# Attention fused with a gated FFN: the global rows one step later, with the second half of the next chunk's scores directly behind them

**Chip, cores, metric.** One NeuronCore of a Trainium2 chip. The metric is the device time of one execution in microseconds, the median of several; all runs compared here were in the fast state, so none lies more than 1.5% above the fastest of its kernel (or they were single looks, whose state is called unknown), with a granted TensorE clock of 0.998 to 1.0.

## The reference

Attention over 8 batches x 8 heads x 576 positions x 64, with a band of 32 positions to each side and 8 "global" positions that see all and are seen by all; then a gated FFN over the 4608 rows of 512.

```python
scores = q @ k.T / sqrt(64)
mask   = (|i - j| <= 32) | is_global[i] | is_global[j]
x      = softmax(where(mask, scores, -1e9)) @ v            # (4608, 512), heads side by side
ffn    = (gelu(x @ w_gate) * (x @ w_val)) @ w_out          # 512 -> 1536 -> 512
out    = x + sigmoid(x @ w_res) * ffn
```

## The kernel before

The 4608 rows are nine chunks c of 512. While TensorE does the FFN of chunk c, the attention of chunk c+1 is woven into the FFN's output half, as jobs ahead of its sixteen steps. Those steps are, for each of four row tiles t: `gate` (four matmuls `r_ps`, then a tanh) and three `third` (four matmuls `f_ps` each; after the last one VectorE makes `prb`). Cut to what matters (`...` marks cuts):

```python
psm = tile_pool(bufs=4, PSUM)   # "mm": g_ps, v_ps, r_ps, f_ps, scores of heads 4..7, in turn
pss = tile_pool(bufs=2, PSUM)   # "sc": ss, scores of heads 0..3, transposes
psn = tile_pool(bufs=1, PSUM)   # "nd": sg, sn, nd take turns in one tile of two banks

def global_scores(b):           # at the end of the input half
    sg = psn.tile(...)          # global queries against all keys
    for hf in range(2):
        for p in range(NP):     # 32 output rows each: the array in strips of 128*32
            nc.tensor.matmul(sg[32*p:32*p+32, hf, 0:288], kgz[b % 2][:, p, :], qt[b % 2][:, p, ...])
    ss = ...                    # all keys against the global queries, 128*128, 20 matmuls
def global_exp(b, sg, ss): ...  # exp(ss) -> ptg, exp(sg) -> gt, and gt *= maskr on VectorE
def global_rows(b):             # "the global rows"
    sn = psn.tile(...)
    for c in range(-1, 5):
        for p in range(NP):     # outputs of 32 or 16 rows: the array in strips of 128*32
            nc.tensor.matmul(sn[32*p:...], own or ptg, vgb or ve, ...)
    nc.vector.tensor_tensor(vgs, sn, head8, ALU.mult)
def scores(c, quad):            # half of a chunk's scores
    for pp in (0, 1):
        sc = two tiles of pss (pp = 0) or of psm (pp = 1)
        heads(c, quad, pp, sc)  # 16 matmuls of 64 rows and 64 columns: the array in halves of 64*128
    four times: nc.scalar.activation(pt, sc, ACTF.Exp, ...)
    return mask                 # later: pt *= maskw on VectorE
def values(c, t):               # nd = pt @ v (16 matmuls, L575), + gt @ vgs (L587); then xtok = nd / den

        jobs = {n: [] for n in range(16)}
        if c + 1 < NCH:
            if held is not None:                               # c = 1 .. 6
                jobs[0].append(lambda: global_exp(b, *held))
                jobs[3].append(lambda: global_rows(b))
            ...
            jobs[1] += [lambda: half(0), lambda: held_mask[0](0, 4)]
            for t in range(4):
                jobs[5 + 2 * t].append(lambda t=t: values(c + 1, t))
                jobs[7 + 2 * t].insert(0, lambda t=t: turn_x(c + 1, t))   # xtok -> xt, t < 3 by DMA
            jobs[5].append(lambda: half(1))
            jobs[6].append(lambda: held_mask[1](0, 2))
            jobs[7].append(lambda: held_mask[1](2, 4))
        for n in range(16):
            for w in jobs[n]:
                w()
            work_f[n]()
```

The softmax here doesn't subtract the row's maximum and nothing guards it: scores larger than these inputs give would overflow.

## Time and profile before

| | before |
|---|---|
| first three runs | 394.37 us (393.6 to 395.18) |
| span of the profiled run | 392.0 us |
| TensorE, VectorE, ScalarE, GpSimd busy | 97%, 52%, 44%, 43% |
| first `r_ps` of chunk c to that of chunk c+1, c = 1 to 5 | 40.48, 40.80, 40.47, 40.81, 40.48 us |

The lines are in the prediction. The last row, the *pitch* of a chunk, is read off TensorE's timeline and will carry the argument: single executions of one kernel differ by over a microsecond, while the pitches of chunks 1 to 5 repeat to 0.02 us in a second trace of each kernel (e5 and e6). How to read a stream of matmuls: take the start of one group to the start of the next, since the printed durations overlap. What such a step has beyond the matmuls' own time where the array's shape changes is called the *toll*.

### The profile page before, as it was taken

How to read it: one execution, taken by the hardware profiler on the slowest of the kernel's cores; microseconds unless marked ns; L12 is line 12 of the kernel's file. 1: busy time of each engine (PE TensorE's matmuls, PEld its weight loads, DVE VectorE, ACT ScalarE, POOL GpSimd, SP SyncE). 2: the span in 40 equal slices, each digit the busy share in tenths (PEclk: the TensorE clock that was granted, in tenths of full speed). 3: DMA queues.
4: the chain of work that ended last, by engine and by line, in shares of the span. 5: the costliest groups of instructions: out<-in, count | busy, mean ns of one | idle time of the engine just before them, and what ended most of it. 6: DMA issues, size and time to landing. Idle time of an engine off the chain costs nothing.

```text
span 392.0 us, 8491 instructions
## 1 busy us (share of the span) xinstructions
PE 378.8 (97%) x3360; PEld 196.5 (50%) x3360; DVE 203.4 (52%) x446; ACT 171.1 (44%) x285; POOL 169.2 (43%) x203
## 2 busy tenths in 40 slices
PE   3989989999999999999999999999999999999996
PEld 2674555444644454445544554455445544554444
DVE  7767773547543664357444644555445534553422
ACT  6753685236333633354335533462337233633321
POOL 7878764958265424561466137712501210121012
PEclk9999999999999999999999999999999999999999
DMA  8999999699759913997399829992990310041002
GB/s 245 256 378 358 239 321 207 149 196 152 110 97 151 184 42 110 122 204 82 88 149 185 88 82 131 189 113 80 114 150 16 81 55 0 2 93 57 0 28 81
DMA packets 153002, 52.78 MB, mean 135 GB/s; under 512 B 136386, under 2 KB 143426, under 8 KB 152962
## 3 DMA queue, kind: packets, MB, share of 16 engines
q1 hardware_dynamic: 77024, 41.88, 44.4%
q0 software_dynamic: 75392, 9.84, 43.0%
q8 instruction: 26, 0.43, 0.5%
q10 hardware_dynamic: 546, 0.52, 0.4%
q14 instruction: 14, 0.11, 0.1%
HBM read 39.19 MB, written 9.44 MB: 124 GB/s over the span
## 4 chain that ended last, share of the span: by engine, by line
PE 93%; DVE 3%; ACT 2%; issue 1%; POOL 0%; DVEq 0%; POOLq 0%; ACTq 0%
PE g_ps L630 24%; PE v_ps L630 23%; PE f_ps L686 23%; PE r_ps L656 8%; PE nd L575 4%; PE sc L534 3%; PE nd L587 2%; PE ss L481 1%; PE sg L472 1%; PE tx L610 1%; PE tk L451 1%; PE sc L523 1%; PE tq L451 1%; ACT pt L541 1%; PE sn L510 1%
## 5 line engine op out<-in xcount | busy, mean ns | idle before, releaser
L639 DVE SCALAR_TENSOR_TENSOR ht<-gsb,v_ps 128x512 bf16<-128x512 bf16 x108 | 74.2, 688 | 95.3 <-PE v_ps L630 89.2
L636 ACT ACTIVATE gsb<-g_ps 128x512 bf16<-128x512 f32 x108 | 64.4, 597 | 123.1 <-PE g_ps L630 119.7
L692 POOL TENSOR_TENSOR ob<-prb,xtok 128x512 f32<-128x512 f32 x35 | 40.3, 1155 | 172.0 <-DVE prb L690 172.0
L630 PE MATMUL g_ps<-xt,wg_t 128*128 128x512 bf16 (+1 forms) x456 | 111.9, 368 | 0.0
L630 PE MATMUL v_ps<-xt,wv_t 128*128 128x512 bf16 (+1 forms) x456 | 111.9, 368 | 0.0
L686 PE MATMUL f_ps<-wo_t,ht 128*128 128x512 bf16 x420 | 100.1, 379 | 0.0
L630 PEld LDWEIGHTS <-wv_t 128*128 128x128 bf16 x456 | 43.4, 98 | 49.1
L630 PEld LDWEIGHTS <-wg_t 128*128 128x128 bf16 x456 | 43.3, 98 | 48.9 <-issue 0.3
L686 PEld LDWEIGHTS <-ht 128*128 128x128 bf16 x420 | 38.9, 98 | 38.9
L664 ACT ACTIVATE rsb<-r_ps 128x512 bf16<-128x512 f32 x36 | 21.5, 600 | 71.8 <-PE r_ps L656 71.8
L690 DVE SCALAR_TENSOR_TENSOR prb<-rsb,f_ps 128x512 f32<-128x512 bf16 x35 | 24.0, 686 | 27.5 <-PE f_ps L686 26.0
L656 PE MATMUL r_ps<-wr_t,xt 128*128 128x512 bf16 x144 | 36.8, 379 | 1.0 <-ACT rsb L664 1.0
L541 ACT ACTIVATE pt<-sc 128x512 bf16<-128x512 f32 x64 | 33.3, 615 | 4.9 <-PE sc L534 4.8
L91 POOL DMA_DIRECT2D q_st<-in_q_dram x25 | 21.5, 866 | 18.5 <-DMA qt<-q_st 18.4
L557 DVE TENSOR_TENSOR pt<-pt,maskw 128x512 bf16<-128x512 bf16 x56 | 23.2, 424 | 7.7 <-ACT pt L541 5.8
L575 PEld LDWEIGHTS <-pt 128*128 128x128 bf16 x576 | 22.0, 97 | 9.5 <-PE r_ps L656 0.7
L99 POOL DMA_DIRECT2D ve<-in_v_dram x30 | 25.5, 866 | 0.0
L600 DVE TENSOR_TENSOR xtok<-nd,rden 128x512 bf16<-128x512 f32 x34 | 23.5, 691 | 1.3
L91 POOL DMA_DIRECT2D k_st<-in_k_dram x25 | 21.1, 864 | 4.8 <-DMA kt<-k_st 4.1
L575 PE MATMUL nd<-ve,pt 128*128 128x65 bf16 x320 | 22.5, 193 | 0.6 <-DVE xtok L600 0.6
L599 DVE RECIPROCAL rden<-nd 128x8 f32<-128x8 f32 x34 | 7.0, 207 | 29.3 <-PE nd L587 29.2
L656 PEld LDWEIGHTS <-xt 128*128 128x128 bf16 x144 | 13.5, 97 | 16.0 <-issue 0.9
(174 smaller groups left out, 307.9 us busy)
## 6 DMA issues: line engine op xcount, KB each, us to landing
out_dram<-ob SPq DMA_DIRECT2D x35, 256.0 KB
vo<-ve SPq DMA_DIRECT2D x12, 260.0 KB
q_st<-in_q_dram POOLq DMA_DIRECT2D x20, 128.0 KB, 5.8
k_st<-in_k_dram POOLq DMA_DIRECT2D x20, 128.0 KB, 6.5
ve<-in_v_dram POOLq DMA_DIRECT2D x18, 128.0 KB, 7.0
wo_t<-in_k_dram SPq DMA_DIRECT2D x8, 256.0 KB
vraw<-in_q_dram SPq DMA_DIRECT2D x8, 256.0 KB
extra<-in_moe_w_out_dram SPq DMA_DIRECT2D x4, 512.0 KB
```

The source lines that it names most:

```text
L91: nc.gpsimd.dma_start(dst[0:n, r, :].rearrange("p (h d) -> p h d", d=D), src[b].rearrange("h s d -> s h d")[128 * r:128 * r + n])
L99: nc.gpsimd.dma_start(t[p0:p1, c, :, 0:D], v[b].rearrange("h s d -> s h d")[s0 + p0:s0 + p1])
L541: nc.scalar.activation(sc if stay else mine, sc, ACTF.Exp, bias=0.0, scale=SCALE)
L575: nc.tensor.matmul(nds[h // 4][:, VG * (h % 4):VG * (h % 4) + VG], view(pt, 0, 128, c0, [[1, 128]]), vw, start=(h % 4 == 0 and e == 0), st ...
L600: nc.vector.tensor_tensor(xtok[c % 2][:, t, :].rearrange("p (a h d) -> p a h d", a=2, d=D), num[:, :, :, 0:D], view(rden, 0, 128, 0, [[4, ...
L630: nc.tensor.matmul(held[what][:, c0:c1], w[:, kk, 128 * j:128 * j + 128], x[:, kk, c0:c1], start=(kk == 0), stop=(kk == NKT - 1))
L636: nc.scalar.activation(held["s"], held["g"], ACTF.Gelu, bias=0.0, scale=1.0)
L639: nc.vector.scalar_tensor_tensor(ht[:, j, :], held["s"], 0.5, held["v"], ALU.mult, ALU.mult)
L656: nc.tensor.matmul(r_ps, xt[c % 2][:, kk, 128 * t:128 * t + 128], wr_t[:, kk, :], start=(kk == 0), stop=(kk == NKT - 1))
L686: nc.tensor.matmul(held["f"], ht[:, j, 128 * t:128 * t + 128], wo_t[:, j, :], start=(j == 0), stop=(j == NFF - 1))
L690: nc.vector.scalar_tensor_tensor(prb, held["r"], 1.0, held["f"], ALU.add, ALU.mult)
L692: nc.gpsimd.tensor_tensor(ob, prb, xtok[c % 2][:, t, :], ALU.add)
```

## The change

The global rows of chunk c+1 move from ahead of step 3 to ahead of step 4, and the second half of the scores from step 5 to directly behind them. In TensorE's order both small groups now stand side by side, with more room between the exps and the rows that need them.

```diff
--- before.py
+++ after.py
@@ -937,7 +937,7 @@
         if c + 1 < NCH:
             if held is not None:
                 jobs[0].append(lambda: global_exp(b, *held))
-                jobs[3].append(lambda: global_rows(b))
+                jobs[4].append(lambda: global_rows(b))
             held_mask = {}
 
             def half(quad):
@@ -947,7 +947,7 @@
             for t in range(4):
                 jobs[5 + 2 * t].append(lambda t=t: values(c + 1, t))
                 jobs[7 + 2 * t].insert(0, lambda t=t: turn_x(c + 1, t))
-            jobs[5].append(lambda: half(1))
+            jobs[4].append(lambda: half(1))
             jobs[6].append(lambda: held_mask[1](0, 2))
             jobs[7].append(lambda: held_mask[1](2, 4))
         for n in range(16):
```

## The prediction

> **What bounds the kernel now.** I read the page first (busy times, slices, groups), then who waited for whom on TensorE, then the timelines of TensorE, VectorE and ScalarE through the FFN output half of single chunks, which is the only place that the diff touches.
>
> ```profile
> span 392.0 us, 8491 instructions
> PE 378.8 (97%) x3360; PEld 196.5 (50%) x3360; DVE 203.4 (52%) x446; ACT 171.1 (44%) x285; POOL 169.2 (43%) x203
> PE   3989989999999999999999999999999999999996
> PEclk9999999999999999999999999999999999999999
> PE 93%; DVE 3%; ACT 2%; issue 1%; POOL 0%; DVEq 0%; POOLq 0%; ACTq 0%
> ```
>
> TensorE is busy for 97% of the span at full clock and holds 93% of the chain that ended last; no other engine is above 52%. The list of waits for TensorE names only one-off waits, nearly all of the start-up (3.5 us the longest); none recurs once per chunk. So the time can change only by what TensorE's own stream costs, or by a wait that the new order creates. I next look inside that stream, in the chunk whose output half starts at 214.37 us (columns: start, duration from first start to last end, instruction group; repeated lines of L575, sixteen in all, cut):
>
> ```profile
> 214.37 1.02 PE L656 MATMUL r_ps<-wr_t,xt 128*128 128x512 bf16 x4
> 215.33 0.64 PE L534 MATMUL sc<-qt,kt 64*128 64x64 bf16 x32
> 215.90 1.90 PE L686 MATMUL f_ps<-wo_t,ht 128*128 128x512 bf16 x8
> 217.73 0.24 PE L507 MATMUL sn<-vgb,own 128*32 128x130 bf16 x4
> 217.80 0.46 PE L510 MATMUL sn<-ve,ptg 128*16 128x130 bf16 x20
> 218.19 1.04 PE L686 MATMUL f_ps<-wo_t,ht 128*128 128x512 bf16 x4
> 219.06 1.03 PE L656 MATMUL r_ps<-wr_t,xt 128*128 128x512 bf16 x4
> 219.93 0.19 PE L575 MATMUL nd<-ve,pt 128*128 128x65 bf16 x1
> ...
> 220.41 0.39 PE L587 MATMUL nd<-vgs,gt 128*128 128x260 bf16 x2
> 220.73 0.64 PE L534 MATMUL sc<-qt,kt 64*128 64x64 bf16 x32
> ```
>
> Read the differences of the starts, not the durations, which overlap. Four 512-column matmuls take 219.93 - 219.06 = 0.87 us, so 0.216 each. The same four before the scores take 215.33 - 214.37 = 0.96: 0.10 more. Eight before the global rows (`sn`) take 217.73 - 215.90 = 1.83, where 8 x 0.216 = 1.73: again 0.10. The two of L587 before the scores take 0.32; the same two before an f_ps group elsewhere in this chunk take 0.22 (223.53 to 223.75): again 0.10. Leaving such a group costs as much. The last of the 20 `sn` matmuls starts at 217.80 + 0.46 - 0.22 = 218.04 (0.22 is one `sn` matmul), its 130 columns need 0.055 at that rate, yet the next group starts at 218.19: 0.10. The last score matmul starts at 215.33 + 0.64 - 0.19 = 215.78, needs 0.03, and the next starts at 215.90: 0.09. So each time the shape of the array changes (128*128 to 64*128 or to 128*32, or back) the stream loses about 0.10 us. This "idle" is inside what the page counts as busy.
>
> **What the Trainium skill says.** TensorEngine Tiling (Array Packing), section Key Properties: changing the tiling mode, not merely the tile, drains the engine. It gives no time; the trace agrees, at 0.09 to 0.10 us a change as just worked out. Perfetto Trace Analysis, section Tensor Engine Instruction: the end of a matmul in a profile is computed, not observed; that is why I count from starts. ScalarE: Activation LUTs, section What ACT_TABLE_LOAD costs: about 1283 ns; here it is 1.28 us (below), and it matters in the last changed chunk.
>
> **The change part by part.** It applies to seven of the nine chunks (c = 1 to 7); the moved global rows exist in six (c = 1 to 6), as the last has no further batch. No instruction is added or removed. TensorE's order in a chunk was: r, sc, f, f, **sn**, f, r, nd, **sc**, f... and becomes: r, sc, f, f, f, **sn, sc**, r, nd, f... I count the changes of shape. Before: r to sc, sc to f, f to sn, sn to f, nd to sc, sc to f: six. After: r to sc, sc to f, f to sn, sn to sc, sc to r: five. Both small groups now stand together and share one change (128*32 straight to 64*128). Does a change between two small shapes cost one toll or none? Chunk 0 has one, in the other direction:
>
> ```profile
> 52.05 0.64 PE L534 MATMUL sc<-qt,kt 64*128 64x64 bf16 x32
> 52.62 0.24 PE L507 MATMUL sn<-vgb,own 128*32 128x130 bf16 x4
> ```
>
> The last score starts at 52.05 + 0.64 - 0.19 = 52.50 and `sn` at 52.62, the same 0.12 as from scores to f_ps: one ordinary toll. So one toll of 0.10 us is saved in each of six chunks: 6 x 0.10 = 0.6 us.
>
> **New waits, c = 1 to 6.** VectorE works in program order, and there prb of the first row tile now comes before vgs (the copy of `sn`):
>
> ```profile
> 216.64 1.90 DVE L557 TENSOR_TENSOR pt<-pt,maskw 128x512 bf16<-128x512 bf16 x4 [0.52 <-ACT pt L541]
> 218.46 0.69 DVE L514 TENSOR_TENSOR vgs<-sn,head 128x520 bf16<-128x520 f32 x1
> 219.33 0.69 DVE L690 SCALAR_TENSOR_TENSOR prb<-rsb,f_ps 128x512 f32<-128x512 bf16 x1 [0.18 <-PE f_ps L686]
> ```
>
> New times in the same chunk, worked out: f_ps (12) from 215.90 to 218.49, toll to 218.59, `sn` to 219.05 (0.46 with its exit), scores to 219.62 (0.57), r to 220.48, then nd. prb starts 0.27 after its last f_ps slot ends (before: 219.33 against 219.06), so at 218.76, when the masks are done (218.54), and ends at 219.45; vgs runs until about 220.14. The nd matmuls need vgs finished, as `sn` and nd share one PSUM tile: 220.14 against 220.48, a margin of 0.3 us. No wait, but close. The scores' four PSUM tiles were last read by the first half's exps, done at 218.07 (215.99 + 2.08 on ScalarE): no wait at 219.05. After values of tile 0 there is now no score group before the next values: 1.73 us of f_ps against the 0.21 + 0.21 + 0.04 + 0.69 us that VectorE needs to empty nd: no wait.
>
> **c = 7.** Without global rows, four changes stay four (r-sc, sc-f, nd-sc, sc-f become r-sc, sc-f, f-sc, sc-r): no toll saved. But here ScalarE is late, as the table load is not hidden under the previous half:
>
> ```profile
> 337.06 1.28 ACT L541 ACT_TABLE_LOAD   x1
> 338.36 2.06 ACT L541 ACTIVATE pt<-sc 128x512 bf16<-128x512 f32 x4
> 340.58 0.60 ACT L664 ACTIVATE rsb<-r_ps 128x512 bf16<-128x512 f32 x1 [0.16 <-PE r_ps L656]
> ```
>
> The chain that ended last leaves TensorE here: exps to 340.42, a mask 0.44, and nd waits until 340.94, 0.27 us inside its group. The new order delays nd past this, so that wait goes. But the psm ring has four buffers: r, sc, sc, f, and then, in the new order, sc, sc and r. The new r takes the buffer of the first half's fourth score tile, free only when the fourth exp ends, at 340.44. TensorE reaches it at 339.51 + 0.10 + 0.57 = 340.18 and waits 0.27. Then r to 341.31, nd 0.71 to 342.02, f_ps at 342.02; before, f_ps started at 342.02 too. Net 0.
>
> **Sum:** 394.37 - 6 x 0.10 - 0 = 393.8 us (span 392.0 to 391.4).
>
> **Rivals.** (1) *A wait on vgs takes the saving back.* prb ahead of vgs leaves 0.3 us of margin; if vgs ends 0.5 us later than I reckon, nd waits 0.2 six times, +1.2 us: 395.0. For it: the semaphore lags are only read off to about 0.1 us. Against: all durations are in the trace and VectorE is otherwise idle there. (2) *Small shapes follow each other free.* `sn` uses column strips and the scores row halves; if their change is free, two tolls go: 393.2. Against: the chunk 0 lines above. (3) *The change frees a real dependency* (exp to global rows, ScalarE under less pressure): a gain of microseconds. Against it: `sn` starts at 217.73, while gt's mask product ended at 216.12, so it waits for nothing now; the page shows no recurring wait to remove. (4) *The late exps in c = 7 gain or lose* up to 0.3 us, if the ring of buffers turns otherwise than I count. (5) Nothing at all: 394.4.
>
> **Range and chances.** All mechanisms together span 393.2 to 395.0. The three runs of before already span 393.6 to 395.18, so the reading itself adds about half a microsecond: 392.9 to 394.8. Two per cent is 7.9 us, some 13 times the expected gain, and more than every wait that I can construct; the chances outside are for the unforeseen.
>
> **What would show it.** TensorE's timeline after: `sn` directly followed by sc, the sc group 0.12 to 0.15 us behind the last `sn` start; 0.22 instead of 0.32 us for the two L587 matmuls of tile 0; r_ps starts of consecutive chunks about 0.1 us closer. prb before vgs on VectorE, vgs ending 0.3 us before nd starts. In c = 7 the 0.27 us gap inside nd gone and one like it before r_ps. Wrong would be: a wait of nd on vgs in every chunk, the same chunk pitch, or a gain beyond 1.5 us.

## The result

| | before | after |
|---|---|---|
| median of 6 runs | 394.27 us | 393.62 us |
| span of the profiled run | 391.95 | 391.35 |
| pitches c = 1 to 6 | 40.48, 40.80, 40.47, 40.81, 40.48, 39.72 | 40.37, 40.70, 40.37, 40.69, 40.37, 39.61 |
| pitch c = 7 | 39.26 | 39.78 |
| first `r_ps` of chunk 0 | 50.22 | 49.75 |

The ratio is 0.9987, 95% interval 0.9965 to 1.0008. (A ratio is the mean time of one kernel's runs over that of the other's of the same rounds, so not quite the ratio of the medians.) The clock alone thus shows no gain in these first rounds. The page's head after, and TensorE's timeline through the same chunk (start, duration, group):

```profile
span 391.4 us, 8491 instructions
```

```profile
213.59 1.02 PE L656 MATMUL r_ps<-wr_t,xt 128*128 128x512 bf16 x4
214.54 0.64 PE L534 MATMUL sc<-qt,kt 64*128 64x64 bf16 x32
215.11 2.76 PE L686 MATMUL f_ps<-wo_t,ht 128*128 128x512 bf16 x12
217.81 0.24 PE L507 MATMUL sn<-vgb,own 128*32 128x130 bf16 x4
217.88 0.46 PE L510 MATMUL sn<-ve,ptg 128*16 128x130 bf16 x20
218.26 0.64 PE L534 MATMUL sc<-qt,kt 64*128 64x64 bf16 x32
218.84 1.04 PE L656 MATMUL r_ps<-wr_t,xt 128*128 128x512 bf16 x4
...
220.20 0.39 PE L587 MATMUL nd<-vgs,gt 128*128 128x260 bf16 x2
220.42 1.89 PE L686 MATMUL f_ps<-wo_t,ht 128*128 128x512 bf16 x8
```

The scores start at 218.26, 0.14 us behind the last `sn` start (217.88 + 0.46 - 0.22 = 218.12), about as f_ps did before (0.15). The two L587 matmuls take 220.42 - 220.20 = 0.22 instead of 0.32: the toll at that place is gone, and no new one has come. VectorE's part, `prb` ahead of `vgs` as foreseen:

```profile
217.99 0.69 DVE L690 SCALAR_TENSOR_TENSOR prb<-rsb,f_ps 128x512 f32<-128x512 bf16 x1 [0.24 <-PE f_ps L686]
218.59 0.69 DVE L514 TENSOR_TENSOR vgs<-sn,head 128x520 bf16<-128x520 f32 x1
```

vgs ends at 219.28; nd starts at 219.71, in its turn. The pitches of chunks 1 to 6 are each shorter by 0.10 to 0.12 us, 0.65 in all. But the traces differ elsewhere too: the start-up was 0.47 us quicker, and chunk 7 took 0.52 us longer. So the agreement of the two spans with the forecast (0.6 less) is partly luck: -0.47 - 0.65 + 0.52 = -0.60. The longer chunk 7 shows as the one new entry of weight in TensorE's list of waits (total, times, longest):

```profile
PE g_ps L630 <- DMA xt<-xtok: 0.4, 1, 0.4
```

(Counted by starts it is 0.55 us; the list counts from the printed, later end of the matmul before.) The prediction has no such wait. Whether the change made it was a question for the experiments.

### The profile page after: what moved, and what is told of

It reads as the page before. It is cut to its first block, busy times and chain, and to the rows that moved or that the text cites. A ratio compares the mean times of both kernels' runs of the same rounds, so it can differ in the third digit from the quotient of the medians.

```text
span 391.4 us, 8491 instructions
## 1 busy us (share of the span) xinstructions
PE 377.8 (97%) x3360; PEld 196.8 (50%) x3360; DVE 201.2 (51%) x446; ACT 170.2 (43%) x285; POOL 168.2 (43%) x203
## 4 chain that ended last, share of the span: by engine, by line
PE 93%; DVE 3%; ACT 2%; DMA 1%; issue 1%; SPq 0%; POOL 0%; DVEq 0%; POOLq 0%; ACTq 0%
PE g_ps L630 24%; PE v_ps L630 23%; PE f_ps L686 22%; PE r_ps L656 8%; PE nd L575 5%; PE sc L534 2%; PE nd L587 2%; PE ss L481 1%; PE sg L472 1%; PE tx L610 1%; DMA xt<-xtok 1%; PE sc L523 1%; PE tk L451 1%; PE tq L451 1%; ACT pt L541 1%
## 5 line engine op out<-in xcount | busy, mean ns | idle before, releaser
L686 PE MATMUL f_ps<-wo_t,ht 128*128 128x512 bf16 x420 | 99.0, 379 | 0.0
L686 PEld LDWEIGHTS <-ht 128*128 128x128 bf16 x420 | 40.0, 98 | 39.5
L557 DVE TENSOR_TENSOR pt<-pt,maskw 128x512 bf16<-128x512 bf16 x56 | 22.4, 421 | 7.1 <-ACT pt L541 5.8
```

The costliest lines, as they stand in the source:

```text
L686: nc.tensor.matmul(held["f"], ht[:, j, 128 * t:128 * t + 128], wo_t[:, j, :], start=(j == 0), stop=(j == NFF - 1))
```

## Experiments

**Theory.** Each change of the array's shape costs TensorE about 0.11 us; the change makes five of six in each of chunks 1 to 6, and nothing else. **Rivals:** the later global rows, or the earlier scores, free some dependency; the wait for xt is the change's doing.

**e1: the rows alone.**

```diff
-            jobs[4].append(lambda: half(1))
+            jobs[5].append(lambda: half(1))      # after values, as before the change
```

> Only the global rows move to step 4; the second half of the scores stays behind the values of tile 0. Toll theory (a change of array shape costs TensorE 0.10 to 0.11 us): the shapes change six times a chunk, as before, so no toll is saved. It also predicts a new wait: without the scores between, nd follows vgs too soon. From the changed kernel's chunk: sn ends at 218.26, r_ps to 219.12, vgs ends at 219.28, so nd waits about 0.2 us in each of six chunks. Time: before + 1.2, about 395.5 us; the pitch of the r_ps starts 40.67 instead of 40.47 us. Rival (the later global rows are what helps, through a dependency): the gain of the changed kernel stays, about 393.6 us.

Measured: 395.9 us, ratio 1.0051 (1.0034 to 1.0067); pitches 40.68, 40.99, 40.67, 41.00, 40.66, so 0.2 over the kernel before. TensorE, then VectorE:

```profile
220.31 0.46 PE L510 MATMUL sn<-ve,ptg 128*16 128x130 bf16 x20
220.70 1.04 PE L656 MATMUL r_ps<-wr_t,xt 128*128 128x512 bf16 x3
221.77 0.19 PE L575 MATMUL nd<-ve,pt 128*128 128x65 bf16 x1
```

```profile
221.02 0.69 DVE L514 TENSOR_TENSOR vgs<-sn,head 128x520 bf16<-128x520 f32 x1
```

Four r_ps matmuls (one record is missing) need 0.86; nd comes after 1.07, 0.06 behind the end of vgs at 221.71. The list of waits doesn't name it, as it is short; the starts show it. So moving the rows alone costs a wait, and the rival "later rows help" is out. The second half of the scores also *covers* the copy of `sn`. The clock shows more than was expected, though: 2.0 us (1.3 to 2.6) over the kernel before, where six waits of 0.2 make 1.2. Its profiled run also started its first r_ps at 51.28 us, the latest of all traces, and waited 0.18 us at the end of chunk 7; whether more than chance lies behind the rest is not shown.

**e2: the scores alone.**

```diff
-                jobs[4].append(lambda: global_rows(b))
+                jobs[3].append(lambda: global_rows(b))
```

> Only the second half of the scores moves to step 4; the global rows stay at step 3, so a group of f_ps stands between the two. Toll theory: six changes of shape, as before, no wait added: pitch 40.47 us in chunks 1 to 5, time as before (394.3 us); in chunk 7 the wait inside nd is replaced by one before r_ps as in the changed kernel. Rival (the earlier scores are what helps): the gain of the changed kernel, pitch 40.37.

Measured: 394.42 us, ratio 1.0017 (1.0 to 1.0033); pitches 40.48, 40.80, 40.47, 40.80, 40.47: those of the kernel before, to 0.01 us. Only both moves together gain.

**e3: the opposite move.** From the kernel before, the rows go *forward*, behind the first half of the scores:

```diff
-                jobs[3].append(lambda: global_rows(b))
...
             jobs[1] += [lambda: half(0), lambda: held_mask[0](0, 4)]
+            if held is not None:
+                jobs[1].append(lambda: global_rows(b))
```

> The opposite move: global rows forward to step 1, directly behind the FIRST half of the scores; the second half stays at its old place. Toll theory: again five changes of shape instead of six, so the same saving as the changed kernel, pitch 40.37 us, about 0.65 us in all, 393.6 us. Rival (more distance between the exps and the global rows helps): nothing gained or a loss, pitch 40.47 or more, as the rows now come 1.8 us sooner after their exps.

Measured: 393.88 us, ratio 1.0 (0.9982 to 1.0019); pitches 40.37, 40.70, 40.36, 40.71, 40.37, the same as the change's. The clock could not show 0.65 us here (its interval is 0.7 to either side); the trace does. Here the toll that goes is the one between scores and f_ps:

```profile
215.77 0.64 PE L534 MATMUL sc<-qt,kt 64*128 64x64 bf16 x32
216.34 0.24 PE L507 MATMUL sn<-vgb,own 128*32 128x130 bf16 x4
216.41 0.46 PE L510 MATMUL sn<-ve,ptg 128*16 128x130 bf16 x20
216.80 2.76 PE L686 MATMUL f_ps<-wo_t,ht 128*128 128x512 bf16 x11
```

(One of the twelve f_ps records is missing.) Two opposite moves with the same saving leave no dependency to explain it: only the number of shape changes is common to both. Nor does every change of group cost: from `r_ps` to `nd`, both 128*128, the step is 0.87 us for four matmuls, without a toll (219.06 to 219.93 in the prediction's lines).

What the toll consists of is a question that these runs do not settle. The weight loads (PEld) of the same chunk of the kernel before:

```profile
215.32 0.35 PEld L534 LDWEIGHTS <-kt 64*128 64x128 bf16 x20 [0.42 <-issue]
219.71 0.38 PEld L575 LDWEIGHTS <-pt 128*128 128x128 bf16 x4
```

The first load of `nd` starts 0.22 us before its matmul (219.93), while r_ps still runs; the first load of the scores starts only 0.01 us before its matmul (215.33). This lead is at most 0.01 us at every change of shape in chunks 1 to 6 of both traces, before and after: there the weights are not loaded ahead. Whether the 0.1 us is the emptying of the array or a weight load (0.10 us long in the profile) that is no longer hidden, no run here separates; the count of changes is the same for both.

**e4: more of the suspected cost.** The second half of the scores in four groups; the last three behind single r_ps matmuls (the helper code is left out):

```diff
                 nc.tensor.matmul(r_ps, ...)
+                if hooks:
+                    hooks.pop(0)()               # eight of the 32 score matmuls; after the last, the exps
```

> The changed kernel with the second half of the scores cut into four groups of eight matmuls, the last three behind the first, second and third r_ps matmul: the same instructions, six more changes of shape in each of seven chunks, 42 in all. Toll theory at 0.105 us: +4.4 us over the changed kernel, about 398.0 us, pitch 41.0 us instead of 40.37. Rival (the saving came from something else than the changes of shape): within 1 us of the changed kernel.

Measured: 398.05 us, ratio 1.0113 (1.009 to 1.0137); pitches 41.01, 41.33, 41.00, 41.34, 41.00: 0.64 over the changed kernel for six changes, 0.106 each. In its timeline one score group of eight takes 0.23 us from start to next start, and an r_ps matmul before scores 0.32 instead of 0.216:

```profile
221.02 0.39 PE L670 MATMUL r_ps<-wr_t,xt 128*128 128x512 bf16 x1
221.34 0.29 PE L534 MATMUL sc<-qt,kt 64*128 64x64 bf16 x8
221.57 0.39 PE L670 MATMUL r_ps<-wr_t,xt 128*128 128x512 bf16 x1
```

**e5 and e6: both kernels again,** for what is chance. No edit.

> The changed kernel once more, for the interval and for the end of chunk 7. In its first trace the first g_ps of chunk 8 waited 0.39 us for the DMA transpose of xt, which landed at 353.19 us; in the kernel before, it landed at 353.79 with the last f_ps just done. If this wait is the change's doing, it comes again: about 39.8 us from the r_ps of chunk 7 to that of chunk 8. If it is chance (a transpose that meets an instruction fetch), it can be anything between 39.2 and 39.8. Pitches of chunks 1 to 5 as before it: 40.37 and 40.70. Time 0.998 of the kernel before.

> The kernel before once more, for its trace alone: pitches 40.48 and 40.80 us again; where the last transpose of xt lands against the last f_ps of chunk 7, and when the first r_ps starts (50.22 us in its first trace), show how much of the two traces' difference is chance.

Measured: the changed kernel 393.86 us against 394.75 in the same rounds, ratio 0.9973 (0.9951 to 0.9994), pitches 40.37, 40.69, 40.37, 40.70, 40.37, 39.61 and, for chunk 7, 39.23. The kernel before, one run, 394.73 us: pitches 40.48, 40.80, 40.49, 40.80, 40.48, 39.73, and chunk 7 *40.01*, with this in its list of waits:

```profile
PE g_ps L630 <- DMA xt<-xtok: 0.6, 1, 0.6
```

So the wait for xt at the end of chunk 7 comes and goes in both kernels: it is not the change's doing. From the landing event of the last DMA transpose of xt in each trace (the last update of its semaphore), and the starts of the last f_ps (plus 0.216) and the first g_ps, the wait is:

| trace | before | e6 | after | e5 | e1 | e2 | e3 | e4 |
|---|---|---|---|---|---|---|---|---|
| wait, us | 0.05 | 0.79 | 0.55 | 0 | 0.18 | 0 | 0.27 | 0.55 |
| g_ps after the landing, us | 0.14 | 0.14 | 0.14 | 0.48 | 0.14 | 0.14 | 0.14 | 0.14 |

In seven of the eight, g_ps starts exactly 0.14 us after the landing: this transpose binds or just ties, whereas at the end of chunks 1 to 6 the landing lies 1.5 to 1.8 us ahead in all eight. The start-up is chance as well: in the changed kernel the first r_ps of chunk 0 starts at 49.75 us in one trace and at 50.95 us in the other (49.75 to 51.28 over all fourteen). From there to the first r_ps of chunk 8 the cleanest pair, before and e5, took 324.42 and 323.74 us: 0.68 less.

**e7: the wait in chunk 7.** The prediction had chunk 7 at net zero, one wait of 0.27 us replaced by another. Both kernels (TensorE; before, then after):

```profile
339.51 1.03 PE L656 MATMUL r_ps<-wr_t,xt 128*128 128x512 bf16 x4
...
341.13 0.39 PE L587 MATMUL nd<-vgs,gt 128*128 128x260 bf16 x2
341.45 0.64 PE L534 MATMUL sc<-qt,kt 64*128 64x64 bf16 x32
342.02 1.25 PE L686 MATMUL f_ps<-wo_t,ht 128*128 128x512 bf16 x5
```

```profile
334.26 1.03 PE L656 MATMUL r_ps<-wr_t,xt 128*128 128x512 bf16 x4
...
338.49 0.76 PE L534 MATMUL sc<-qt,kt 64*128 64x64 bf16 x32
339.35 1.02 PE L656 MATMUL r_ps<-wr_t,xt 128*128 128x512 bf16 x4
340.70 0.39 PE L587 MATMUL nd<-vgs,gt 128*128 128x260 bf16 x2
340.92 1.89 PE L686 MATMUL f_ps<-wo_t,ht 128*128 128x512 bf16 x8
```

After, the scores take 0.86 us from start to next start instead of 0.58: the last of them starts at 338.49 + 0.76 - 0.19 = 339.06, nearly in its turn, and the r_ps behind them only at 339.35, just as the first half's fourth exp has ended (339.31 in the chain of waits). So the gap lies before r_ps, where the prediction put it. From the chunk's first r_ps to this f_ps it is 342.02 - 335.38 = 6.64 before and 340.92 - 334.26 = 6.66 after: net zero. e7 takes the cause away:

```diff
         jobs = {n: [] for n in range(16)}
+        if c == NCH - 2:                          # chunk 7: load the table of exp before its first tanh
+            jobs[0].append(lambda: nc.scalar.activation(none, none, ACTF.Exp, bias=0.0, scale=1.0))
```

> The changed kernel, and in chunk 7 alone a one-column exp on ScalarE at the head of the output half, so that the table load runs while ScalarE waits for r_ps. Buffer theory of chunk 7 (the second half of the scores and the second r_ps wait 0.28 us for the first half's exps, which the table load of 1.28 us delays): the exps start over 1 us sooner, both waits go, scores take 0.58 instead of 0.86 us, and the f_ps of step 5 comes 6.38 us after the r_ps of the chunk instead of 6.66. Rival (the 0.28 us has another cause, such as the change of shape): 6.66 stays.

Measured, one look: 392.93 us. ScalarE and TensorE:

```profile
334.71 1.28 ACT L938 ACT_TABLE_LOAD   x1
336.01 0.20 ACT L938 ACTIVATE none<-none 128x1 f32<-128x1 f32 x1
336.12 0.58 ACT L664 ACTIVATE rsb<-r_ps 128x512 bf16<-128x512 f32 x1
336.60 2.05 ACT L541 ACTIVATE pt<-sc 128x512 bf16<-128x512 f32 x4
```

```profile
338.99 0.64 PE L534 MATMUL sc<-qt,kt 64*128 64x64 bf16 x32
339.56 1.04 PE L656 MATMUL r_ps<-wr_t,xt 128*128 128x512 bf16 x4
...
341.15 1.89 PE L686 MATMUL f_ps<-wo_t,ht 128*128 128x512 bf16 x8
```

0.57 us for the scores, and 341.15 - 334.76 = 6.39 to the f_ps, as expected: the late table load was the cause.

**e8 and e9: the last transpose.**

```diff
-        if c > 1 and t < 3:
+        if c > 1 and t < (2 if c == NCH - 1 else 3):    # last chunk: tile 2 on TensorE too
```

> The changed kernel, with the third transpose of xt for the last chunk on TensorE (four small matmuls and a copy on VectorE) instead of the DMA. Theory that the landing of the last DMA transpose releases the first g_ps of chunk 8: that wait goes, at the price of 0.22 us for the four matmuls; from r_ps of chunk 7 to the first g_ps 18.8 to 18.9 us instead of 19.06. Rival (something else held g_ps back): 19.3.

> The changed kernel with the early table load and with the third transpose of the last chunk on TensorE. If both theories hold, chunk 7's output half (r_ps to first g_ps of chunk 8) takes 19.06 - 0.28 - 0.2 = 18.6 us, and the whole about 0.45 us less than the changed kernel, 0.997 of the kernel before. If the landing still binds (the second transpose is late too), 18.8 or more.

Measured: e8 (one look) 393.73 us, and 18.73 us from chunk 7's r_ps to the first g_ps of chunk 8, with g_ps 1.3 us after the landing of the last DMA transpose left: no wait. But its chunk 5 (pitch 40.49) ends with a wait of 0.12 us, g_ps again 0.14 us after the landing of an xt transpose. e9: 18.45 us, and 393.66 us, ratio 0.9971 (0.9947 to 0.9994); its chunk 2 took 0.17 us longer than in e5, since `ss` took 0.68 us instead of 0.51 to the next start: one of its matmuls waited 0.15 us for a DMA transpose of kt. With DMA transposes that stretch took 18.51 (e5) to 19.06 us (after). So the transpose on TensorE costs 0.22 us and removes, at this one place, a wait of 0 to 0.55 us seen in traces of the changed kernel. Between e5 and e9, in the same rounds, the clock shows no difference, neither the 0.45 us expected nor steadier times (393.02 to 395.22 us against 392.83 to 394.56).

**e10 to e12: toward a better version.** If shape changes are what counts, another can go: sg, in strips, stands between v_ps and ss.

```diff
-        sg = psn.tile(...)  # and its eight matmuls, in global_scores
+        sg = global_sg(b) if b < 2 else None
...
+            if held is not None:
+                jobs[1].append(lambda: rows_exp(b, global_sg(b)))   # sg, exp(sg) and its mask
             jobs[1] += [lambda: half(0), lambda: held_mask[0](0, 4)]
```

> The changed kernel, and the rows' global scores sg (eight matmuls in 128*32 column strips, with their exp) move from ahead of ss and the first r_ps to directly before the first half of the scores. Changes of shape from the last v_ps on: before v to sg, sg to ss, r to sc, then as in the changed kernel; now r to sg, sg to sc: one fewer. Toll theory: another 0.106 us in each of six chunks, pitch 40.26 and 40.59 instead of 40.37 and 40.70 us, 0.64 us in all: 0.9965 to 0.997 of the kernel before. Rival (the 0.11 us of the change was peculiar to sn behind f_ps): pitch unchanged.

> The kernel of e10 with the early table load of chunk 7 as well: from the first r_ps of chunk 1 to that of chunk 8 about 323.74 - 0.64 - 0.28 = 282.0 us less the 42.4 of chunk 0, that is 240.4 us, plus up to 0.4 if the last transpose lands late; about 1.6 us below the kernel before, 0.996 of it.

> The three additions together on the changed kernel: sg directly before the first half of the scores, the early table load of chunk 7, and the third transpose of the last chunk on TensorE. In ten of the thirteen traces so far the first g_ps of chunk 8 starts 0.14 us after the landing of the last transpose, having waited up to 0.79 us; with that transpose on TensorE it should not wait: from r_ps of chunk 7 to the first g_ps 18.45 us as in e9. From the first r_ps of chunk 0 to that of chunk 8: 323.74 (the changed kernel without a wait) - 0.64 - 0.28 + 0.22 = 323.0 us, plus 0.1 to 0.4 if a transpose of kt or xt lands late elsewhere. Time 0.995 to 0.996 of the kernel before, no clear difference from e11.

(The text for e11 has a slip of the pen: 323.74 - 0.64 - 0.28 is 322.8, and that is the whole stretch from chunk 0 to chunk 8.)

Measured for e10, TensorE:

```profile
213.51 0.65 PE L485 MATMUL ss<-qgz,kt 128*128 128x16 bf16 x20
214.01 1.02 PE L665 MATMUL r_ps<-wr_t,xt 128*128 128x512 bf16 x4
214.96 0.43 PE L472 MATMUL sg<-qt,kgz 128*32 128x288 bf16 x8
215.32 0.64 PE L543 MATMUL sc<-qt,kt 64*128 64x64 bf16 x32
```

| | ratio to before, 95% | pitches c = 1 to 5 | chunk 0 to chunk 8 |
|---|---|---|---|
| e5 (the change) | 0.9973 (0.9951 to 0.9994) | 40.37 40.69 40.37 40.70 40.37 | 323.74 |
| e10 | 0.9965 (0.9945 to 0.9985) | 40.26 40.59 40.26 40.67 40.44 | 323.64 |
| e11 | 0.9957 (0.9937 to 0.9977) | 40.26 40.60 40.70 40.59 40.35 | 323.35 |
| e12 | 0.9969 (0.9948 to 0.9991) | 40.26 40.59 40.26 40.59 40.38 | 323.17 |

The further toll is saved where nothing else stands in the way (40.26 and 40.59 against 40.37 and 40.70). But it is often given back: in e10 chunk 5 ends with a wait of 0.11 us for an xt transpose that lands late, chunk 4 with one of 0.08 us, 0.25 us behind such a landing, and chunk 7 with one of 0.29 us, and 0.07 us more are lost inside the scores of chunk 5, by what is not seen; in e11 the earlier ss of chunk 3 waits 0.28 us for a DMA transpose of kt (0.42 by the starts). So of the 0.64 us expected of e10 its trace keeps 0.10, and e11 lies 0.5 us above its corrected 322.8, more than the 0.4 it allowed for. Whether landings bind more often because TensorE runs faster is not shown: e8 and e9, without this move, have one such wait each. Medians were 393.63, 393.36 and 393.46 us. All three beat the kernel before (each interval lies below 1); their intervals overlap with each other's and with the change's own, so a lead over the change is shown by the traces of single executions only.

## Why the prediction was right

- *TensorE's stream alone bounds the time.* Right from the first r_ps on: the differences traced between there and the first r_ps of chunk 8 are shape changes or waits of that stream. The scatter of the start-up was not looked into.
- *One toll of 0.10 us saved in each of six chunks.* Right, and shown by the count of changes, not by the clock of the first rounds; slightly small: 0.10 to 0.12 us a chunk, 0.65 in all instead of 0.6. e2 and e3 show that it is the count of changes, e4 sizes one at 0.106 us over six of them. The step that carried the forecast was the one pair of small groups in chunk 0: a change between two small shapes costs one toll, neither none nor two.
- *vgs still comes in time, with 0.3 us to spare.* Right: 0.43 us (219.28 against 219.71), as vgs starts 0.09 us before the printed end of prb, where the prediction put one behind the other. e1 shows how near the other outcome lay: without the scores between, the wait is there, 0.2 us a chunk, and the kernel is 0.5% slower by the clock.
- *Chunk 7: net zero.* Right, 6.64 against 6.66 us, and by the named cause (e7).
- *What the prediction missed.* It had no wait for the last DMA transpose of xt, though in the trace of before g_ps started 0.14 us after that landing, with 0.05 us of wait. It is worth 0 to 0.79 us from one execution to the next, more than the whole gain, and with the start-up (a spread of 1.5 us over all the traces) it makes most of the scatter that the range allowed for without a cause. The first pair of traces agreed with the forecast partly because these two offset each other, which was luck. The range was also narrower than its own working: it ends at 394.8 us, below the 395.0 us of rival 1, and allows half a microsecond for the reading where the first three runs spanned 1.6. And the second half's four score tiles were not all last read by the first half's exps: by the ring that the prediction counts for chunk 7, one took the buffer of r_ps, which is free earlier, so nothing follows from it.
- *The rivals.* The wait on vgs and the free change of shape did not come (pitch 40.37, not 40.57 or 40.26); a freed dependency is excluded by e1 to e3.

What stays open: what the toll consists of (after e3), and why the last transposes of chunk 7 land so differently. In the traces of before, e6 and after, the two issues in a row took SyncE 3.66, 3.00 and 4.18 us, against 2.52 in the earlier chunks, and a 16 KB packet of the queue that the page calls "instruction" moves during the longer of the two. That the two collide is argued from this coincidence, not shown: no run took the packet away. Nor does the length of the issues order the waits: e6 has the shortest of the three and the longest wait (0.79 us), before has 3.66 us and a wait of 0.05.

## What to carry to other kernels

When TensorE is 97% busy and waits for nothing, read the starts of its groups: the loss can sit between groups of different array shape, at 0.1 us for each change here, and changes are saved by putting small-tile groups side by side. Before doing so, check what the group that used to stand between was covering (here a copy out of PSUM) and which buffers the reordered groups take in turn. And for gains of a tenth of a per cent compare repeating intervals inside the traces, since the clock needs many runs to see what a pitch shows in one trace; but look for a late DMA in that pitch first, since one of them can hide the gain (e8, e10, e11).

## What the Trainium skill lacked or had wrong

- TensorEngine Tiling (Array Packing), Key Properties: it says that a change of tiling mode drains the engine, but gives no price, and not that the weights of the new mode are then loaded only 0.01 us ahead of their matmul (0.22 us between groups of one mode). Here 0.106 us per change (six extra changes a chunk, pitch 41.01 against 40.37 us), and one such price between 128*32 or 128*16 and 64*128 as well (40.37 in e3 and in the change). Inside `sn`, where the recorded shape goes from 128*32 to 128*16, no such step is seen: the first four matmuls and the twenty after them start 0.07 us apart.
- Perfetto Trace Analysis, Tensor Engine Instruction: that the ends of matmuls are computed is right, and it could add that the time lost between modes is therefore counted as busy (97% here, with eight such gaps a chunk in the kernel before, the two around sg included).
- ScalarE: Activation LUTs, What ACT_TABLE_LOAD costs: the load itself agrees, 1.28 us in every trace. The drain of about 1.38 us that the page adds, 2.66 us in all for each switch, is not seen here: in chunk 7 of before the tanh ends at 336.45 + 0.60 = 337.05 and the first exp starts at 338.36, 1.31 us later and right behind the load.
- No page that we read tells how far the landing of an SBUF-to-SBUF DMA transpose scatters: here, with one kernel on unchanged data, it held the first matmul of the last chunk back by 0.05 and 0.79 us (before and e6), or by 0.55 and 0 us (after and e5).
